# Retention states by full-array products from the second batch on, and the last sums in pieces

## The chip, the cores and the metric

The kernel runs on one core of a Trainium2 chip. The core has five engines with their own instruction streams: PE (TensorE, matrix products into PSUM), DVE (VectorE), ACT (ScalarE), POOL (GpSimd) and SP (SyncE, here only for transfers), and 16 DMA engines. The metric is the device time of one execution in microseconds, as a median of several. Engines work in the order of their streams and wait for each other through semaphores.

## The reference

Two layers follow each other: a recurrent retention over 768 steps and 8 heads, then an MLP mixer with a token part and a channel part. There are 4 batches; a head has 64 columns.

```python
gamma = 1.0 - 2.0 ** (-5.0 - np.arange(H))                 # one decay per head
for t in range(S):                                          # S = 768
    state = gamma[None, :, None, None] * state + np.einsum('bhd,bhe->bhde', k[:, :, t], v[:, :, t])
    y[:, :, t] = scale * np.einsum('bhd,bhde->bhe', q[:, :, t], state)
x  = y.transpose(0, 2, 1, 3).reshape(B, S, H * D)           # 4 x 768 x 512
h  = np.maximum(x.T @ w_tok1, 0) @ w_tok2                   # per batch, along the tokens, 256 wide
u  = x + h.T
h2 = np.maximum(u @ w_ch1, 0) @ w_ch2                       # along the channels, 1536 wide
out = u + h2
```

## The kernel before

The 768 steps are cut into 6 chunks of 128. Two heads form a pair (4 pairs a batch), so that a pair fills the 128 partitions. `front(b, p)` does a pair of a batch: it scales k by powers of gamma, transposes k and q, forms the states at the chunk borders, the scores inside a chunk, the retention output y, and then the token MLP of these 128 channels; its last product is the transposed u (`uT`). `back(b)` does the channel MLP of a batch from the four `uT`: `widen` (384-column products, L803, Relu on ACT) and `narrow` (512-column products, L845) or, for batches 2 and 3, `narrow_seven` (256-column products, L922), which saves one product in eight by sums and differences formed on DVE.

No order of instructions is written down. Every step is an `Op` with an engine (or a choice of engines), an estimated cost, the steps it depends on, and the buffers it takes from a limited number (`BUFS`) or PSUM banks from a range (`BANKS`). A list scheduler in the kernel places them, with some random changes from seeds, and the best order is emitted. Costs in the code are in nanoseconds: (time to the next instruction, time to the result). In the first 36 us products with zeros (L1049, "filler") are put where PE would stand idle.

```python
BUFS = dict(kf=6, qf=6, k16=3, v16=8, kT=4, qT=4, U=2, q16=3, r16=3, am=8, X=3, x16=5, h1=3, u16=3,
            uT=3, h2=2, o=4, w1=2)
BANKS = dict(first=range(0, 7), front=range(0, 5), back=range(3, 8), seven=range(0, 8), fill=range(7, 8))
QR, QH, TN = (0,), (1,), 2
SEEDS = [30004]
...
def front(b, p):
    first, last = b == 0, b == 0 and p == NP - 1
    turned = first and p >= TN            # these pairs take a shortcut to uT, see below
    FA = "first" if first else "front"
    ...
    ST, US, RS = Slot(FA), Slot("U"), Slot("r16")
    def emit():
        st = tile_of(ST, [P, 512], FP)
        for c in range(NC - 1):           # 5 chunk borders
            for j in range(2):            # 2 heads: 10 products into the two halves of the partitions (L527)
                nc.tensor.matmul(st[j * D:(j + 1) * D, c * D:(c + 1) * D], K.tile[:, c, j],
                                 V.tile[:, j, c], start=True, stop=True)
    pp = op(one("PE", (375, 525), emit), kl + [vl, two_before], [ST], [K, V])
    for c in range(NC - 1):               # U[c] = decay * U[c-1] + state product c, on DVE
        def emit(c=c):
            o = ST.tile[:, c * D:(c + 1) * D]
            if c == 0:
                U = tile_of(US, [P, NC - 1, D], FP)
                nc.vector.tensor_copy(U[:, 0], o)                                   # L536
            else:
                U = US.tile
                nc.vector.scalar_tensor_tensor(U[:, c], U[:, c - 1], gp[:, p:p + 1], o,
                                               ALU.mult, ALU.add)                  # L539
    ...                                   # r16 = U scaled, per head on the diagonal blocks (L550/L552)
    ...                                   # scores (L576), mask (L590), y (L606, L610), X (L624/L628), x16 (L641)
    t1: 12 products x16, wt1 (L655);  h1 = relu
    if turned:                            # uT straight from h1 and x16, and the residual later in narrow
        2 x 2 products of 384 columns (L680) and 2 x 3 of 128 (L683), evicted to uT (L690)
        return
    t2: 12 products of 128 columns (L713); X += t2 on DVE, twice (L720); u16 = cast (L728)
    uT: 6 transposes on PE (L747) and an eviction (L753), or a DMA transpose for batches 2 and 3 (L737)
    ...
def narrow(sh):                           # batch 0: the token residual of the turned pairs, 2 products in each of 6 groups
    nc.tensor.matmul(A.tile[:, TN * P:], wt2[:, jt, t], h1_all[:, jt, TN * P:], ...)   # L835
    ...
def narrow_seven():                       # the end of group i
    p7 = mm(PB, lo, ...)
    u3 = add(W1, lo, ...)                                                           # w<-w,bank
    p2 = mm(PA, lo, ...)
    p3 = mm(PC, hi, sv("S4"), b_of(1, 1), False, True, ...)                         # the last 6 products
    ol1 = add(OL, lo, ...)
    oh = op(either(emit, DVE=(640, 700), POOL=(1250, 1330)), [oh, u3], [], [OH, W1]) # OH += W1, 512 wide (L964)
    ol2 = add(OL, hi, ..., [p3, v12], ...)                                          # 256 wide
    stores = [(1, OH, slice(0, C), [oh]), (0, OL, slice(0, C), [ol1, ol2])]
    if b == B - 1 and i == HC - 1:
        stores[1:] = [(0, OL, lo, [ol1]), (0, OL, hi, [ol2])]                       # all from ACT
```

Of the kernel before, what the change touches and what calls it, by code (L numbers as in the profile page):

```python
# [18 lines left out]
def kernel(  # L19
# [32 lines left out]
    BUFS = dict(kf=6, qf=6, k16=3, v16=8, kT=4, qT=4, U=2, q16=3, r16=3, am=8, X=3, x16=5, h1=3, u16=3,  # L52
# [4 lines left out]
    QR, QH, TN = (0,), (1,), 2  # L57
    SEEDS = [30004]
# [31 lines left out]
    def replay(order):  # L90
# [23 lines left out]
        while n:  # L114
# [51 lines left out]
            for e, o in on:  # L166
# [4 lines left out]
                if left[e] <= 0:  # L171
                    left[e] = None
                    dmas[e].pop(0)
                    o.end = t + LAND[e] + (AFTER if e == "POOL" and t > 50000 else 0)
                    n -= 1
# [248 lines left out]
    def front(b, p):  # L424
# [96 lines left out]
        ST, US, RS = Slot(FA), Slot("U"), Slot("r16")  # L521

        def emit():
            st = tile_of(ST, [P, 512], FP)
            for c in range(NC - 1):
                for j in range(2):
                    nc.tensor.matmul(st[j * D:(j + 1) * D, c * D:(c + 1) * D], K.tile[:, c, j],  # L527
                                     V.tile[:, j, c], start=True, stop=True)
        pp = op(one("PE", (375, 525), emit), kl + [vl, two_before], [ST], [K, V])
        prev = None  # L530
        for c in range(NC - 1):
            def emit(c=c):
                o = ST.tile[:, c * D:(c + 1) * D]
                if c == 0:
                    U = tile_of(US, [P, NC - 1, D], FP)
                    nc.vector.tensor_copy(U[:, 0], o)  # L536
                else:
                    U = US.tile
                    nc.vector.scalar_tensor_tensor(U[:, c], U[:, c - 1], gp[:, p:p + 1], o,  # L539
                                                   ALU.mult, ALU.add)  # L540
            prev = op(one("DVE", (190, 273), emit), [pp, prev], [US] if c == 0 else [],
                      [ST, US] if c else [ST])

        def emit(e, j):
# [4 lines left out]
            if e == "ACT":  # L549
                nc.scalar.mul(RS.tile[r, :, r], US.tile[r], g128[2 * p + j])  # L550
            else:
                nc.vector.tensor_scalar(RS.tile[r, :, r], US.tile[r], g128[2 * p + j], None, ALU.mult)  # L552
# [230 lines left out]
    def back(b):  # L783
# [79 lines left out]
        def narrow_seven():  # L863
# [47 lines left out]
            for i in range(HC):  # L911
# [5 lines left out]
                def mm(bank, cols, lhs, rhs, opens, adds, deps, reads):  # L917
# [6 lines left out]
                    return op(one("PE", (648, 806), emit), deps, [bank] if opens else [],  # L924
                              reads + ([] if opens else [bank]))

                def add(o, cols, a, c, deps, takes, uses, pooled=False, n=N2):
# [4 lines left out]
                    cost = dict(DVE=(640, 700) if n > N2 else (365, 425))  # L932
                    if pooled:
                        cost["POOL"] = (1250, 1330) if n > N2 else (720, 800)
                    return op(either(lambda e: emit(e), **cost), deps, takes, uses)
                xl = [x_done[b, p, 0] for p in range(NP)]
# [20 lines left out]
                p3 = mm(PC, hi, sv("S4"), b_of(1, 1), False, True,  # L957
# [125 lines left out]
```

## Time and profile before

| | |
|---|---|
| time, median of 3 | 200.04 us (199.78 to 203.64) |
| span of the profiled execution | 197.7 us |
| granted PE clock | 0.996 |
| PE, weight loads, DVE, ACT, POOL busy | 95%, 66%, 67%, 56%, 41% |
| chain that ended last: PE, DMA, DVE | 62%, 16%, 12% |
| longest part of it, by line | PE L803 24%, L922 13%, L845 12% |
| stores of 256 KB and of 128 KB, issue to landing | 3.0 us, 2.0 us |

The profile is of one execution. A busy engine is one with an instruction under way; matmuls are pipelined, so the time that one costs in a stream is read from the starts of neighbours and not from its own duration. The groups name line, engine, operation, written and read tiles, shape and count, then busy time, mean duration in ns, and the idle time of the engine before them. A chain of work goes back from the last instruction, at each step to what released it. A timeline lists start, duration, engine, line and how many instructions of a kind were merged.

### The profile page before, as it was taken

Reading aid. Unit: us, or ns where it says so; the run is one execution under the profiler, and the core shown is the slowest. Engines: PE = TensorE matmul, PEld = TensorE weight load, DVE = VectorE, ACT = ScalarE, POOL = GpSimd, SP = SyncE. Lnnn points to the kernel's source line nnn. Section 1 sums busy time; section 2 is a strip of 40 time slices with the busy share of each in tenths; the row PEclk is TensorE's granted clock in tenths of the full one; section 3 lists DMA queues with packets and bytes.
Section 4 is the critical chain, followed back from the end, with each engine's and each line's share of the span. In section 5 each row is a group of like instructions: output and inputs, shape, how many; then the busy total and the mean of one; then the engine's idle time right before and its main releaser. Section 6 shows DMA issues by size and latency. Waiting matters only on the chain.

```text
span 197.7 us, 4974 instructions
## 1 busy us (share of the span) xinstructions
PE 188.0 (95%) x1994; PEld 129.8 (66%) x1994; DVE 131.9 (67%) x343; ACT 111.1 (56%) x244; POOL 80.4 (41%) x114
## 2 busy tenths in 40 slices
PE   7778899999999999999999999999999999999991
PEld 3456686666767656667755764567767787667881
DVE  6699671019799997687668425476399687048972
ACT  4468766899758656469460872439765004775000
POOL 7996765389979874246251220222220010000000
PEclk9999999999999999999999999999999999999998
DMA  7999999999999999999999993452220024000232
GB/s 114 149 170 178 209 204 206 179 155 153 145 145 180 109 167 188 149 172 179 153 131 190 157 170 73 120 122 40 40 45 0 0 107 189 26 0 3 100 114 106
DMA packets 97511, 24.89 MB, mean 126 GB/s; under 512 B 90193, under 2 KB 94545, under 8 KB 97489
## 3 DMA queue, kind: packets, MB, share of 16 engines
q0 software_dynamic: 73136, 13.18, 95.3%
q1 hardware_dynamic: 20752, 5.11, 20.4%
q10 hardware_dynamic: 3600, 6.29, 9.8%
q8 instruction: 15, 0.25, 0.6%
q14 instruction: 8, 0.06, 0.1%
HBM read 26.74 MB, written 6.29 MB: 167 GB/s over the span
## 4 chain that ended last, share of the span: by engine, by line
PE 62%; DMA 16%; DVE 12%; POOL 4%; issue 2%; ACT 2%; DVEq 0%; POOLq 0%
PE bank L803 24%; PE bank L922 13%; PE bank L845 12%; DMA wc<-in_moe_w_ch_dram 9%; DMA kf<-in_k_dram 7%; PE bank L655 3%; PE bank L713 3%; DVE am L590 3%; PE bank L576 2%; PE bank L610 2%; DVE U L539 2%; POOL v L387 2%; DVE X L720 1%; DVE k L467 1%; PE bank L606 1%
## 5 line engine op out<-in xcount | busy, mean ns | idle before, releaser
L803 PE MATMUL bank<-uT,wc 128*128 128x384 f16 x384 | 67.9, 326 | 0.0
L817 ACT ACTIVATE h<-bank 128x384 f16<-128x384 f32 x96 | 45.8, 490 | 20.2 <-PE bank L803 14.3
L803 PEld LDWEIGHTS <-wc 128*128 128x128 f16 x384 | 35.7, 98 | 21.5
L590 DVE TENSOR_TENSOR am<-bank,mask 128x384 f16<-128x384 f32 x64 | 32.6, 548 | 10.3 <-PE bank L576 10.3
L845 PE MATMUL bank<-wc,h 128*128 128x512 f16 x144 | 36.2, 380 | 0.0
L624 ACT ACTIVATE X<-bank,gy 128x192 f32<-128x192 f32 x56 | 19.9, 419 | 17.4 <-PE bank L610 17.1
L641 POOL CAST x<-X 128x384 f16<-128x384 f32 x24 | 12.2, 510 | 27.2 <-ACT X L624 24.6
L728 POOL CAST u<-X 128x384 f16<-128x384 f32 x25 | 12.8, 524 | 23.7 <-DVE X L720 23.1
L720 DVE TENSOR_TENSOR X<-X,bank 128x384 f32<-128x384 f32 x28 | 14.3, 549 | 10.2 <-PE bank L713 10.1
L845 PEld LDWEIGHTS <-h 128*128 128x128 f16 x144 | 12.4, 98 | 10.5
L539 DVE SCALAR_TENSOR_TENSOR U<-U,gp,bank 128x64 f32<-128x64 f32 x64 | 17.6, 276 | 1.2
L387 POOL DMA_DIRECT2D v<-in_v_dram x16 | 16.5, 1031 | 4.4 <-DMA kf<-in_k_dram 2.2
L387 POOL DMA_DIRECT2D kf<-in_k_dram x15 | 15.3, 1021 | 2.2 <-DMA qf<-in_q_dram 0.9
L922 PEld LDWEIGHTS <-h 128*128 128x128 f16 x144 | 14.1, 98 | 1.8
L550 ACT ACTIVATE r<-U 64x320 f16<-64x320 f32 x28 | 13.1, 467 | 3.4 <-DVE U L539 3.0
L610 PEld LDWEIGHTS <-am 128*128 128x128 f16 x192 | 12.3, 98 | 2.5
L610 PE MATMUL bank<-v,am 128*128 128x64 f16 x192 | 13.8, 193 | 0.0
L655 PE MATMUL bank<-x,wt 128*128 128x128 f16 x192 | 13.5, 219 | 0.2 <-DVE am L590 0.2
L655 PEld LDWEIGHTS <-wt 128*128 128x128 f16 x192 | 11.9, 98 | 2.7 <-issue 0.5
L467 DVE TENSOR_SCALAR k<-kf,gk 128x384 f16<-128x384 f16 x14 | 6.2, 447 | 10.5 <-DMA kf<-in_k_dram 10.5
L713 PEld LDWEIGHTS <-wt 128*128 128x128 f16 x168 | 10.5, 98 | 2.6 <-issue 0.5
L713 PE MATMUL bank<-h,wt 128*128 128x128 f16 x168 | 12.0, 219 | 0.1
(91 smaller groups left out, 265.9 us busy)
## 6 DMA issues: line engine op xcount, KB each, us to landing
out_dram<-o ACTq DMA_DIRECT2D x23, 256.0 KB, 3.0
v<-in_v_dram POOLq DMA_DIRECT2D x16, 192.0 KB, 8.7
wc<-in_moe_w_ch_dram POOLq DMA_DIRECT2D x6, 512.0 KB, 15.6
kf<-in_k_dram POOLq DMA_DIRECT2D x15, 192.0 KB, 8.6
qf<-in_q_dram POOLq DMA_DIRECT2D x12, 192.0 KB, 8.7
wt<-in_moe_w_tok_dram POOLq DMA_DIRECT2D x2, 384.0 KB, 9.1
qf<-in_q_dram POOLq DMA_DIRECT2D x8, 96.0 KB, 8.4
X<-in_k_dram SPq DMA_DIRECT2D x1, 384.0 KB, 3.5
```

The lines of the kernel that those rows point to most:

```text
L387: nc.gpsimd.dma_start(out=tile_of(s, [P, 2, NC, D], F16), in_=src[b, 2 * p:2 * p + 2].rearrange("h (c p) d -> p (h c) d", p=P))
L539: nc.vector.scalar_tensor_tensor(U[:, c], U[:, c - 1], gp[:, p:p + 1], o, ALU.mult, ALU.add)
L590: nc.vector.tensor_tensor(am[:, :m], src, k_, ALU.mult)
L610: nc.tensor.matmul(o[:, j * D:(j + 1) * D], M.tile[:, m], V.tile[:, j, c], start=(c == 0), stop=(c == 0 or j == 1))
L624: nc.scalar.mul(X.tile[:, half(hf), h * D:(h + 1) * D], yv[:, :, j * D:(j + 1) * D], gy[:, h:h + 1])
L655: nc.tensor.matmul(acc[:, jt * P:(jt + 1) * P], wt1[:, i, jt * P:(jt + 1) * P], X16.tile[:, i], start=(i == 0), stop=(i == NC - 1))
L713: nc.tensor.matmul(acc[:, i * P:(i + 1) * P], wt2[:, jt, t], H1.tile[:, jt], start=(jt == 0), stop=(jt == NJ - 1))
L720: nc.vector.tensor_tensor(xo, xo, T2.tile[:, :HC * P].rearrange("p (i d) -> p i d", d=P), ALU.add)
L803: nc.tensor.matmul(acc[:, :SH], w[:, ct, (ft % FW) * P:(ft % FW + 1) * P], UT.tile[:, ct, sh * SH:(sh + 1) * SH], start=(ct == 0), stop=(c ...
L817: nc.scalar.activation(H2.tile[:, ft], A.tile[:, :SH], AF.Relu)
L845: nc.tensor.matmul(A.tile, H2.tile[:, ft, i * P:(i + 1) * P], wc2[ft // FW][:, ft % FW], start=(opens and ft == 0), stop=(ft == NF - 1), s ...
L922: nc.tensor.matmul(bank.tile[:, cols], lhs(f, t), rhs(f), start=(f == 0 and not adds), stop=(f == HF - 1), skip_group_check=adds)
```

## The change

From batch 1 on (`UNT = 1`), a pair's state at a chunk border is formed by one product of 128 stationary and 128 moving columns, both heads at once, instead of two products of half the array width. Of its four 64 x 64 blocks two mix the heads and are never used; the U sums carry them along, so U is twice as wide (`UW = P`) and the products fill two PSUM banks instead of one. The aim is fewer, fuller products and no change of the array's tiling. Batch 0 keeps the ten half products. To make room, q gets five buffers and x16 four. `TN` goes from 2 to 3, so that only pair 3 of batch 0 takes the shortcut. In the very last group, the last product and its sum are done in two pieces of 128 columns with a store each, the add of W1 is split between POOL and DVE, and the 256 KB store goes out from SP. Other seeds are tried for the order, so all streams after about 28 us are interleaved differently.

```diff
-    BUFS = dict(kf=6, qf=6, ... x16=5, ...)
+    BUFS = dict(kf=6, qf=5, ... x16=4, ...)
...
+    UNT, UW = 1, P
-    QR, QH, TN = (0,), (1,), 2
-    SEEDS = [30004]
+    QR, QH, TN = (0,), (1,), 3
+    SEEDS = [20002, 20003, 20007, 20226]
...
+        whole = b >= UNT
+        STS = [ST, Slot(FA)] if whole else [ST]
+        W = P if whole else D
+        def st_of(c):
+            return STS[c // 4] if whole else ST
...
             for c in range(NC - 1):
-                for j in range(2):
-                    nc.tensor.matmul(st[j * D:(j + 1) * D, c * D:(c + 1) * D], K.tile[:, c, j],
-                                     V.tile[:, j, c], start=True, stop=True)
-        pp = op(one("PE", (375, 525), emit), kl + [vl, two_before], [ST], [K, V])
+                if whole:
+                    nc.tensor.matmul(st_of(c).tile[:, c % 4 * P:(c % 4 + 1) * P],
+                                     K.tile[:, c].rearrange("p h d -> p (h d)"),
+                                     V.tile[:, :, c], start=True, stop=True)
+                else:
+                    ...                                     # the two half products, as before
+        pp = op(one("PE", (270, 420) if whole else (375, 525), emit), kl + [vl, two_before], STS, [K, V])
...
-                    nc.vector.scalar_tensor_tensor(U[:, c], U[:, c - 1], gp[:, p:p + 1], o,
+                    nc.vector.scalar_tensor_tensor(U[:, c, :W], U[:, c - 1, :W], gp[:, p:p + 1], o,
                                                    ALU.mult, ALU.add)
...
-                nc.scalar.mul(RS.tile[r, :, r], US.tile[r], g128[2 * p + j])
+                nc.scalar.mul(RS.tile[r, :, r], US.tile[r, :, r if whole else slice(0, D)], g128[2 * p + j])
...
+                ends = b == B - 1 and i == HC - 1
+                for cols in ((slice(N2, N2 + P), slice(N2 + P, C)) if ends else (hi,)):
+                    p3.append(mm(PC, cols, sv("S4"), ...))
...
+                if ends:
+                    ohs = [op(either(lambda e, hs=hs, f=emit: f(e, hs), **c), [oh, u3], [], [OH, W1])
+                           for hs, c in ((slice(0, 1), dict(POOL=(720, 800))), (slice(1, 2), dict(DVE=(365, 425))))]
...
+                if ends:
+                    store(0, i, OL, lo, [ol1])
+                    store(1, i, OH, slice(0, C), ohs, "SP")
+                    for n_, (p3_, cols) in enumerate(zip(p3, (slice(N2, N2 + P), slice(N2 + P, C)))):
+                        ol2 = add(OL, cols, ..., [p3_, v12], [], [OL, PC], n=P)
+                        store(0, i, OL, cols, [ol2], "ACT")
```

## Prediction

> **What bounds the kernel now.** I read the page's part 1 and its 40 slices first, then the chain that ended last in order of time, then the PE timeline around the instructions that change. Part 1 and the rows of PE and DVE:
>
> ```profile
> PE 188.0 (95%) x1994; PEld 129.8 (66%) x1994; DVE 131.9 (67%) x343; ACT 111.1 (56%) x244; POOL 80.4 (41%) x114
> ...
> PE   7778899999999999999999999999999999999991
> ...
> DVE  6699671019799997687668425476399687048972
> ```
>
> PE is busy in every slice from about 30 us on. As a busy PE isn't PE at its peak, I checked that its matmuls stand end to end. The chain in order of time, its last third:
>
> ```profile
> 144.03 6.50 PE bank L803 x40
> 150.53 3.27 PE bank L922 x30
> 153.81 1.95 PE bank L803 x12
> 155.76 10.48 PE bank L922 x96
> 166.24 13.65 PE bank L803 x84
> 179.89 11.80 PE bank L922 x108
> 191.71 0.69 DVE o L931
> ```
>
> Forty products of 384 columns in 6.50 us are 0.1625 us each, and 108 of 256 columns in 11.80 us are 0.109: the columns at 2.4 GHz plus some 2.5 ns. Nothing waits here. From the chain and the timeline I take for one full-array product of 128 columns 0.056 us (twelve L655 in 0.67). The first L803 starts at 30.68 us; from there to the last PE product, streaming and mode changes explain all but about half a microsecond of some 163. So the kernel is bound by PE's work after 30.7 us, by what comes before that (loads and dependences), and by a tail of 4 us. PE work removed after 30.7 us comes off the time almost one to one; other engines matter only where they make PE wait.
>
> **What the state products cost.** The PE timeline around one pair's ten products (L527):
>
> ```profile
> 96.54 0.49 PE L803 MATMUL bank<-uT,wc 128*128 128x384 f16 x2
> 96.96 0.35 PE L527 MATMUL bank<-v,k 128*64 128x64 f16 x10
> 97.24 0.50 PE L803 MATMUL bank<-uT,wc 128*128 128x384 f16 x2
> ```
>
> The two L803 should have streamed by 96.54 + 2 x 0.1625 = 96.86, yet L527 starts at 96.96: 0.10 us of gap. The ten themselves take 97.24 - 96.96 = 0.28 us. The 0.38 in all recurs at the other pairs of later batches.
>
> **What the Trainium skill says.** "TensorEngine Tiling (Array Packing)", Key Properties: "Changing tiling mode (not just tile) drains the TensorE". The trace agrees: 0.10 us when the half-width products come after full-width ones. "TensorE: Matmul & The Clock Gate", "Wait — 56ns, not 53.3ns?": 128 columns take 55.6 ns back to back; the trace's 56 agrees. "VectorE: DVE Perf Modes", "Why PSUM operands drop a tier": fp32 operands in PSUM run at one element per cycle. The trace agrees: DVE adds of 256 and 512 columns take 417 and 688 ns (below), 1.06 ns a column. "DMA: Bandwidth & Descriptors", Anatomy of one DMA, puts about 2 us of fixed cost on a transfer; the page's part 6 has stores of 256 KB landing after 3.0 us and of 128 KB after 2.0, so here size counts as well.
>
> **The change part by part.**
>
> 1. State products. Five full-array products of 128 columns: 5 x 0.056 = 0.28 us, with no change of mode. Streaming is thus the same; what goes is the 0.10 us of gap, in 12 pairs (batches 1 to 3): 12 x 0.095 = **-1.13 us** of PE.
>
> 2. The threshold TN goes from 2 to 3: pair 2 of batch 0 no longer goes through the transposed shortcut. PE loses 4 products of 384 (0.65), 6 of 128 (0.34), and in the six narrow groups of batch 0, 12 products shrink from 256 to 128 columns (12 x 0.053 = 0.64). It gains 12 L713 (0.67) and 6 transposes (0.34). Net **-0.62 us** of PE. In exchange DVE gets two adds (L720, 0.47 us each start to start) and POOL two casts.
>
> 3. DVE. The rows:
>
> ```profile
> L539 DVE SCALAR_TENSOR_TENSOR U<-U,gp,bank 128x64 f32<-128x64 f32 x64 | 17.6, 276 | 1.2
> L931 DVE TENSOR_TENSOR o<-o,bank 128x256 f32<-128x256 f32 x6 | 2.5, 417 | 0.3 <-PE bank L922 0.2
> L931 DVE TENSOR_TENSOR o<-X,bank 128x512 f32<-128x512 f32 x6 | 4.1, 688 | 1.0 <-PE bank L922 0.8
> ```
>
> Five instructions a pair get 64 more columns: 5 x 64 x 1.06 = 0.34 us, +4.1 us of DVE over 12 pairs. Where does DVE have no room? By stages of 10 us (columns: PE, PEld, DVE, ACT, POOL busy):
>
> ```profile
> 50.00:60.00 10.00, 9.87 (x135) 6.73 (x134) 8.74 (x23) 5.97 (x13) 8.41 (x11) 1.00 3.63 145
> 60.00:70.00 10.00, 9.82 (x123) 6.63 (x121) 9.77 (x26) 7.43 (x14) 9.20 (x11) 1.00 2.48 145
> ```
>
> So it lies in the front of batch 1, where the chain runs through DVE too (about 52 to 70 us). PE has batch 0's channel MLP to fill in with and didn't wait. The widening of batch 1 starts at 85.1 us; its last transposed input is evicted at 79.7 to 80.2. The changed order asks for it earlier: between the first widening product of batch 0 and that of batch 1 stand 50.5 us of PE work instead of 53.7, so it is due near 81.5. Adding up DVE's instructions from the first scaling of k in batch 1 to the last L720 of that batch gives 26.2 us before and 26.0 after: the scheduler moved other DVE work behind it. So it should hold, with a microsecond to spare instead of five. I put **+0.3 us** on waits of this kind, two PSUM banks per state included.
>
> 4. The head. Until the second L713 group the streams are identical. Then pair 2's L713 group stands where L680 started at 28.54:
>
> ```profile
> 28.54 0.49 PE L680 MATMUL bank<-wt,h_all 128*128 128x384 f16 x2
> ...
> 29.86 0.98 PE L655 MATMUL bank<-x,wt 128*128 128x128 f16 x12
> 30.68 1.14 PE L803 MATMUL bank<-uT,wc 128*128 128x384 f16 x6
> ```
>
> 28.54 + 0.67 = 29.21; six transposes until about 29.67; three filler products until 30.16; L655 waits for a DVE cast that now stands behind pair 2's first add (about 30.2). It starts near 30.3 and not 29.86, so the first L803 near 31.0, with 0.32 us less work done before it (14.64 against 14.96): **+0.6 us** of idle PE.
>
> 5. The tail. The end of the timeline:
>
> ```profile
> 193.55 1.33 ACTq L973 DMA_DIRECT2D out_dram<-o  x3
> 193.76 0.41 DVE L931 TENSOR_TENSOR o<-o,bank 128x256 f32<-128x256 f32 x1
> ```
>
> Three stores were issued one after the other on ACT, some 0.45 us apart; the last at about 194.45, although its add ended at 194.18. After: the 256 KB store goes to SP, but ACT still issues three (128, 64, 64 KB). The first can't go before the left add, which ends 0.3 us earlier as the add with W1 is split between POOL and DVE. The last issue thus stays near 0.7 us after PE's end; the saved part is mostly the smaller last transfer, against the later POOL half (0.73 us). **-0.15 us**.
>
> Sum: -1.13 - 0.62 + 0.3 + 0.6 - 0.15 = -1.0 us, so 200.04 - 1.0 = **199.0 us**.
>
> **Rivals.** (a) DVE becomes the bound in batch 1: each microsecond by which the last input of the widening comes after 81.5 us is one of PE. For it: 9.77 of 10 us busy between 60 and 70. Against it: equal DVE sums to the deadline, and PE's filling work. It would give 200 to 202. (b) The gain is full: no new wait, and the head loses nothing because the filler products only stood where PE waited anyway. Then -1.13 - 0.62 - 0.3 = -2.0, or 198.0. For it: PE waited only half a microsecond after 30.7 us in a schedule made in the same way. (c) The mode changes don't vanish but move: the score products (L576, 64 rows) are left as they are, so where L527 stood directly next to them a gap was shared. In batches 1 to 3 none of the L527 groups stands next to L576 in the trace, so I count nothing. It would halve part 1: 199.6. (d) Fewer buffers (qf 5, x16 4) hold up the POOL queue, which issues loads in order. A load of batch 2 would then wait for a transpose of batch 1 long done; up to +1 us, only if a weight or a k comes late.
>
> **Range and chances.** The gains are counted products with measured durations; the uncertain terms (head, waits, tail) are each some tenths, and rival (a) has a tail upward. 198.0 to 200.7 should hold it 8 times in 10. Faster by over 2% would need 4 us, more than all removed work: 0.02. Slower by over 2% needs a new wait of 5 us: 0.04. Within 2%: 0.94.
>
> **What would show it.** In the profile after: the state products as 60 full-array ones, five in 0.28 us with no gap ahead; U updates of 128 columns about 340 ns long; first L803 equivalent near 31.0 us; the first widening product of batch 1 at 81 to 82 us without a PE wait ahead; PE's last product near 192.9 us; a span near 196.7. I'm wrong if PE waits for DVE or for transposed inputs between 50 and 85 us or near 152 us (batch 3's inputs), if a gap stays at the state products, or if the head differs by over a microsecond.

## The result and the profile after

| | before | after |
|---|---|---|
| time, median of 4 | 199.91 us (199.52 to 203.64) | 197.77 us (197.54 to 198.15) |
| ratio, with 95% interval | | 0.9901 [0.9874, 0.9929] |
| profiled execution: time, span | 199.45, 197.7 us | 198.15, 196.4 us |
| first widening product of batch 0 | 30.68 us | 30.75 us |
| first widening product of batch 1 | 84.93 us | 81.39 us |
| last product of PE starts | 193.37 us | 192.04 us |
| from there to the end of the span | 4.31 us | 4.34 us |

The four executions are faster by 1.0%, about twice what was predicted, and the time lies below the predicted range. First the page of the kernel after, part 1 and the slices of PE and DVE:

```profile
PE 187.0 (95%) x1951; PEld 130.6 (67%) x1951; DVE 132.1 (67%) x338; ACT 112.9 (58%) x251; POOL 82.9 (42%) x118
...
PE   7878899999999999999999999999999999999991
...
DVE  6699682017899998677676726566299686048972
```

PE has 43 instructions fewer, and as before it is busy in every slice from 30 us on. DVE's busy time is the same within 0.2 us in spite of the wider sums. PE's timeline of the kernel after around one pair's state products (L536):

```profile
43.18 0.49 PE L818 MATMUL bank<-uT,wc 128*128 128x384 f16 x2
43.51 0.44 PE L536 MATMUL bank<-v,k 128*128 128x128 f16 x5
43.78 0.65 PE L818 MATMUL bank<-uT,wc 128*128 128x384 f16 x3
```

Two widening products of 0.1625 us from 43.18 have streamed by 43.51, where the five state products start; 0.28 us later the next product starts. The 0.10 us of gap that stood ahead of the ten half products is gone. It is so at every pair: ahead of the twelve groups of batches 1 to 3, the trace before has eleven gaps of 0.093 to 0.095 us and one of 0.133, 1.17 us in all, and the trace after has none above 0.001. The score products with 64 rows, which were left as they are, have a gap of 0.096 us ahead of each of their twelve groups in both traces, so the gaps have not moved there, as rival (c) had it. Over the whole run I summed the time by which each product of PE starts later than its predecessor has streamed, from the first widening product to the last product: 4.39 us before, 3.26 after. (The level depends on the streaming time taken for the half-array products, the difference does not.) The twelve gaps thus account for the whole difference of 1.13 us, and PE's other waits sum to the same in both traces within 0.04 us.

The sums of the states, from the costliest groups of the page:

```profile
L553 DVE SCALAR_TENSOR_TENSOR U<-U,gp,bank 128x128 f32<-128x128 f32 (+1 forms) x64 | 20.9, 327 | 1.5
```

The 327 ns are a mean over two shapes: 48 sums of 128 columns at 345 ns and 16 (batch 0) of 64 columns at 272.

The head, in PE's timeline of the kernel after:

```profile
29.52 0.65 PE L1086 MATMUL bank<-zero 128*128 128x384 f16 x3
30.01 0.90 PE L670 MATMUL bank<-x,wt 128*128 128x128 f16 x12
30.75 0.81 PE L818 MATMUL bank<-uT,wc 128*128 128x384 f16 x4
```

The three filler products (L1086) run from 29.52 to 30.01, and T1 (L670, the first product of the token MLP) starts there: it does not wait for the cast.

### The profile page after: what moved, and what is told of

Same layout as the page of the kernel before. It is cut to its first block, busy times and chain, and to the rows that moved or that the text cites. A ratio compares the mean times of both kernels' runs of the same rounds, so it can differ in the third digit from the quotient of the medians.

```text
span 196.4 us, 4910 instructions
## 1 busy us (share of the span) xinstructions
PE 187.0 (95%) x1951; PEld 130.6 (67%) x1951; DVE 132.1 (67%) x338; ACT 112.9 (58%) x251; POOL 82.9 (42%) x118
## 4 chain that ended last, share of the span: by engine, by line
PE 73%; DMA 12%; DVE 6%; POOL 3%; issue 2%; ACT 1%; ACTq 0%; DVEq 0%; POOLq 0%
PE bank L818 32%; PE bank L937 14%; PE bank L860 9%; DMA qf<-in_q_dram 9%; PE bank L670 4%; PE bank L728 4%; DMA kf<-in_k_dram 3%; DVE am L605 3%; PE bank L591 2%; PE bank L625 2%; PE bank L502 1%; PE bank L621 1%; PE bank L536 1%; DVE U L553 1%; POOL v L388 1%
## 5 line engine op out<-in xcount | busy, mean ns | idle before, releaser
L818 PE MATMUL bank<-uT,wc 128*128 128x384 f16 x384 | 69.3, 326 | 0.0
L656 POOL CAST x<-X 128x384 f16<-128x384 f32 x25 | 12.8, 513 | 29.8 <-ACT X L639 25.9
L639 ACT ACTIVATE X<-bank,gy 128x192 f32<-128x192 f32 x58 | 20.6, 420 | 6.1 <-PE bank L625 5.9
L735 DVE TENSOR_TENSOR X<-X,bank 128x384 f32<-128x384 f32 x30 | 15.8, 550 | 9.9 <-PE bank L728 9.7
L553 DVE SCALAR_TENSOR_TENSOR U<-U,gp,bank 128x128 f32<-128x128 f32 (+1 forms) x64 | 20.9, 327 | 1.5
L743 POOL CAST u<-X 128x384 f16<-128x384 f32 x27 | 13.4, 516 | 17.9 <-DVE X L735 17.7
L564 ACT ACTIVATE r<-U 64x320 f16<-64x320 f32 x31 | 14.5, 467 | 5.9 <-DVE U L553 5.5
L990 POOL TENSOR_TENSOR o<-o,w 128x256 f32<-128x256 f32 x1 | 1.0, 964 | 32.2 <-DVE w L947 32.2
L670 PE MATMUL bank<-x,wt 128*128 128x128 f16 x192 | 13.6, 219 | 0.5 <-DVE am L605 0.3
L670 PEld LDWEIGHTS <-wt 128*128 128x128 f16 x192 | 11.9, 98 | 2.6 <-issue 0.9
L728 PE MATMUL bank<-h,wt 128*128 128x128 f16 x180 | 13.3, 219 | 0.0
L728 PEld LDWEIGHTS <-wt 128*128 128x128 f16 x180 | 11.5, 98 | 2.5 <-issue 0.2
## 6 DMA issues: line engine op xcount, KB each, us to landing
wc<-in_moe_w_ch_dram POOLq DMA_DIRECT2D x6, 512.0 KB, 15.2
```

What stands on the lines that cost most here:

```text
L553: nc.vector.scalar_tensor_tensor(U[:, c, :W], U[:, c - 1, :W], gp[:, p:p + 1], o, ALU.mult, ALU.add)
L639: nc.scalar.mul(X.tile[:, half(hf), h * D:(h + 1) * D], yv[:, :, j * D:(j + 1) * D], gy[:, h:h + 1])
L670: nc.tensor.matmul(acc[:, jt * P:(jt + 1) * P], wt1[:, i, jt * P:(jt + 1) * P], X16.tile[:, i], start=(i == 0), stop=(i == NC - 1))
L728: nc.tensor.matmul(acc[:, i * P:(i + 1) * P], wt2[:, jt, t], H1.tile[:, jt], start=(jt == 0), stop=(jt == NJ - 1))
L735: nc.vector.tensor_tensor(xo, xo, T2.tile[:, :HC * P].rearrange("p (i d) -> p i d", d=P), ALU.add)
L818: nc.tensor.matmul(acc[:, :SH], w[:, ct, (ft % FW) * P:(ft % FW + 1) * P], UT.tile[:, ct, sh * SH:(sh + 1) * SH], start=(ct == 0), stop=(c ...
```

## Experiments

Times are medians with the lowest and highest execution; ratios are to the kernel before on the same chip, with a 95% interval. The ratios leave out executions more than 1.5% above the fastest of their kernel, so they can differ from the ratio of the medians.

### Are the products' gains what the gap says?

**Ten half-array products and 64-column sums again, in the new order.**

```diff
-                if whole:
-                    nc.tensor.matmul(st_of(c).tile[:, c % 4 * P:(c % 4 + 1) * P],
-                                     K.tile[:, c].rearrange("p h d -> p (h d)"), V.tile[:, :, c], ...)
-                else:
+                if True:                                    # the two half products, in all batches
...
-                nc.vector.scalar_tensor_tensor(U[:, c, :W], U[:, c - 1, :W], ...)
+                nc.vector.scalar_tensor_tensor(U[:, c, :D], U[:, c - 1, :D], ...)
```

> The changed kernel's order of instructions on every engine, but in batches 1 to 3 the states again by ten half-width products, with U 64 wide. Theory (PE-bound, the gap of a change of tiling costs 0.095 us a pair): 1.1 us above the changed kernel, and a gap of 0.10 us ahead of each of the 12 groups. Rival (the gain comes from the other order of the scheduler and from TN, not from the states): within 0.3 us of the changed kernel. Rival (DVE's wider U costs time): less than 0.8 us above, as DVE gets back 4 us.

Measured: 200.01 us (199.36 to 201.61), 1.0009 [0.9993, 1.0026]. So the order, `TN` and the new end seem to bring nothing alone. But PE's timeline shows a wait that the changed kernel does not have:

```profile
58.28 0.60 PE L856 MATMUL bank<-wc,h 128*128 128x512 f16 x2
59.76 0.45 PE L666 MATMUL bank<-x,wt 128*128 128x128 f16 x5 [0.88 <-DVE U L549]
```

T1 waits for the last sum of a pair, and 1.05 us pass between the streams. In this version all five states of a pair lie in one PSUM bank; in the changed kernel the fifth is in a second bank, so I take it that the bank T1 needs comes free one sum earlier there. The sum on DVE is what the trace names; the bank is my reading of the code. It fits that in the changed kernel T1 starts ahead of that last sum:

```profile
58.60 0.83 PE L670 MATMUL bank<-x,wt 128*128 128x128 f16 x12
...
59.44 0.34 DVE L553 SCALAR_TENSOR_TENSOR U<-U,gp,bank 128x128 f32<-128x128 f32 x1
```

The wait is thus one of this experiment, which keeps an order made for two banks. Without it the version would stand near 199.0 us (an estimate, 200.01 less 1.05), so it doesn't show that the rest of the change brings nothing.

**Ten full-stationary products of 64 columns**: the count of the old kernel with the tiling of the new.

```diff
                 if whole:
-                    nc.tensor.matmul(st_of(c).tile[:, c % 4 * P:(c % 4 + 1) * P], K..., V.tile[:, :, c], ...)
+                    for j in range(2):
+                        nc.tensor.matmul(st_of(c).tile[:, c % 4 * P + j * D:c % 4 * P + (j + 1) * D], K..., V.tile[:, j, c], ...)
```

> Order of the changed kernel; each of the five full products as two of 64 moving columns with the whole stationary matrix: ten products and ten weight loads, the same columns streamed, no change of tiling. Theory (tiling change is what costs): as the changed kernel, within 0.3 us, no gap ahead of the group, ten in 0.28 us or little more. Rival (the number of products and weight loads costs): 1 us or more above, ten taking 0.37 us or more.

Measured: 199.67 us (198.13 to 203.41), 0.9972 [0.9946, 0.9997]; the spread is the subject of a later part. Its traced execution took 202.99 us at a granted clock of 0.987, so only the places of its products are read. PE's timeline at a pair:

```profile
72.46 0.59 PE L861 MATMUL bank<-wc,h 128*128 128x512 f16 x2
72.89 0.45 PE L537 MATMUL bank<-v,k 128*128 128x64 f16 x10
73.18 0.59 PE L861 MATMUL bank<-wc,h 128*128 128x512 f16 x2
```

Two products of 512 columns of 0.215 us from 72.46 end at 72.89, where the ten start; they take 0.29 us. No gap, although there are ten; at eleven of the twelve pairs there is none, at one 0.05 us. What the change saves is the change of tiling and not the number of products.

### The end

**The old end of the last sums** (DVE adds all of the right half, no pieces, stores from ACT):

```diff
-                ends = b == B - 1 and i == HC - 1
+                ends = False
```

> The changed kernel with the old end: last product in one piece, W1 added at once on DVE, all three last stores from ACT. Prediction: 0.15 us slower than the changed kernel. From the trace (last product's end to the end of the span 4.20 us before, 4.29 after): 0.05 to 0.1 us faster, since ACT still issues three stores one after the other and the last one goes at the same distance from PE's end.

Measured: 199.29 us (197.48 to 201.20), 0.9946 [0.9922, 0.9971]. The median says little, again because of the spread, but in the trace the last product is followed by 4.29 us to the end of the span, against 4.34 and 4.32 in two traces of the new end. The new end saves nothing.

**The very last piece stored from SP** instead of as the third issue on ACT (with the moved loads of the version with late k and v below):

```diff
-                        store(0, i, OL, cols, [ol2], "ACT")
+                        store(0, i, OL, cols, [ol2], "SP" if n_ else "ACT")
```

> The first variant of this call, and the very last piece's store goes out from SP, so that ACT issues two stores at the end instead of three. The last ACT issue started 1.10 us after the last product's start with DVE done at 0.74. Theory: the last issue starts near 0.8 us, the end comes 0.25 to 0.35 us earlier: 197.5 to 197.9. Rival (the end is set by the transfers, not by the issues): no difference.

Measured: 199.53 us (197.83 to 201.76), 0.9946 [0.9913, 0.9979]; from the last product to the end 4.32 us, no change. So the third issue on ACT isn't what ends the kernel. In the timeline of the kernel after, the end is:

```profile
191.47 0.96 POOL L990 TENSOR_TENSOR o<-o,w 128x256 f32<-128x256 f32 x1 [32.16 <-DVE w L947]
...
192.21 1.32 ACTq L955 DMA_DIRECT2D out_dram<-o  x3
...
192.46 0.36 SPq L955 DMA_DIRECT2D out_dram<-o  x1
```

The 256 KB store (SPq) can't go before POOL's half ends, at 192.43. It goes 0.42 us after the last product's start (192.04); before, it went first from ACT, 0.18 after. It is not the last to land, though: it is through at 194.64, and the third store of ACT at 195.15. That one is issued 1.10 us after the last product's start, before as after, and its size doesn't matter here. Stores of the end, KB each and us to landing, before and then after:

```profile
out_dram<-o ACTq DMA_DIRECT2D x2, 128.0 KB, 2.0
```

```profile
out_dram<-o ACTq DMA_DIRECT2D x2, 64.0 KB, 2.1
```

The very last took 1.91 us with 128 KB and 2.02 with 64. With its issue from SP, 0.23 us earlier, it landed 3.11 us after the last product's start, as in the changed kernel. So at the end the landings are what counts; that the later 256 KB store holds up the small ones behind it is likely and not shown.

### Has DVE room?

**One more copy of 128 columns on DVE for each state sum** (five a pair, into a tile that nobody reads):

```diff
                     nc.vector.scalar_tensor_tensor(U[:, c, :W], U[:, c - 1, :W], ...)
+                if whole:
+                    nc.vector.tensor_copy(dump, o)
```

> The changed kernel with one more DVE copy of 128 x 128 beside each state sum of batches 1 to 3 (0.2 us each, 1 us a pair, three times what the change itself added), otherwise the same order. Prediction's rival (DVE near its limit in batch 1): PE waits appear between 70 and 85 us, 2 us or more above the changed kernel. My reckoning (DVE had about a microsecond to spare): about 1 to 3 us above. If DVE has wide slack: within 0.5 us.

Measured: 201.12 us (200.67 to 202.37), 1.0053 [1.0028, 1.0078]. DVE is busy 141.2 us instead of 132.1, some 0.8 us a pair more, and PE's gaps sum to 6.6 us instead of 3.26. After 31 us PE waits for the extra copy to read its bank, a wait that the changed kernel does not have:

```profile
PE bank L594 <- DVE dump L557: 0.7, 2, 0.4
...
PE bank L765 <- DVE dump L557: 0.2, 1, 0.2
```

Beside them stand 0.3 us for a sum on DVE and 0.5 for a Relu on ACT. So a bound by DVE, rival (a), is near: over twice the change's own 0.34 us a pair is too much, while that 0.34 still fits.

### The spread

**The changed kernel again**, and later four more traces of it.

> The changed kernel again, for a second trace and a narrower interval. By the trace in hand the span fell 1.3 us (1.13 of it the gaps at the state products, the rest other PE work) while the medians fell by 2.1. If the trace is typical, the difference narrows to 1.3 to 1.6 us (ratio 0.992 to 0.9935). If the trace in hand was one of the slower executions of the changed kernel, the difference stays near 2 us (0.989 to 0.991) and the new trace shows where, most likely before the first widening product (30.75 us so far).

Measured: 199.41 us (197.74 to 199.94), 0.9957 [0.9925, 0.9989]. The eleven times are 197.74, 197.90, 198.00, 198.27, 198.37 and then 199.41 to 199.94: two groups with nothing between. The four recorded times all lie in the lower one. The four later traces:

> The changed kernel once more, for its trace. Holding back the scaling of k did not remove the upper group of executions, so its cause is open. If this execution falls into the upper group (199.3 us or more), its trace shows where it departs from the lower one: before the first widening product (beyond 31.2 us: the loads at the start), between 50 and 85 us (a PE wait of 1 to 2 us), or later. If it is of the lower group (197.5 to 198.6), it repeats the traces in hand.

> As the first run of this call, the changed kernel for another trace. Upper group: one of the three places; lower group: first widening product at 30.7 to 31.2 us and no PE wait above 0.4 us after it.

> As the first run of this call, the changed kernel for another trace. Upper group: one of the three places; lower group: first widening product at 30.7 to 31.2 us and no PE wait above 0.4 us.

> As the first run of this call, the changed kernel for another trace. Upper group: one of the three places; lower group: first widening product at 30.7 to 31.2 us and no PE wait above 0.4 us.

Measured: 199.71, 200.75, 199.48 and 199.68, all in the upper group or above it, at a granted clock of 0.995 to 1.0 as in the lower. All four ran on one chip, and the eleven above on another, so the group may go with the chip; that was not tried. Now the upper group can be read. Its own PE gaps sum to 5.4 to 5.8 us against 3.26 and 3.10 in the two traces of the lower group. In the first of them the 2.31 us over the recorded trace are 0.70 at 41 to 45 us, about 1.1 between 75 and 78, and 0.5 between 82 and 84. The first cancels against the head: in this trace the first widening product stands at 29.97 us, 0.8 earlier than in the recorded one, and PE then gives it back in waits, 0.3 us of them for a load of q. The rest is the upper group's loss. In the waits of ACT between 70 and 86 us, first the recorded trace, then the first of the four:

```profile
ACT k L466 <- DMA kf<-in_k_dram: 1.1, 1, 1.1
ACT q L475 <- DMA qf<-in_q_dram: 0.9, 1, 0.9
```

```profile
ACT k L466 <- DMA kf<-in_k_dram: 2.1, 1, 2.1
...
ACT q L475 <- DMA qf<-in_q_dram: 1.4, 1, 1.4
```

DVE waits for its half of the same k: 0.5 us in the recorded trace, 1.6 in the other. These are k and q of batch 2's last pair, issued by POOL at 60.5 and 61.5 us in both. k landed 14.0 us later in the recorded trace and 15.0 in the other, q 18.1 and 19.7 us later. Loads of this size issued between 36 and 60 us take 7 to 9. What stands behind them in ACT's stream, in the recorded trace and then in the upper one:

```profile
79.67 0.83 ACT L475 COPY q<-qf 128x768 f16<-128x768 f16 x1 [0.89 <-DMA qf<-in_q_dram]
...
80.41 1.35 ACT L639 ACTIVATE X<-bank,gy 128x192 f32<-128x192 f32 x4
```

```profile
81.20 0.83 ACT L475 COPY q<-qf 128x768 f16<-128x768 f16 x1 [1.41 <-DMA qf<-in_q_dram]
...
81.94 1.35 ACT L639 ACTIVATE X<-bank,gy 128x192 f32<-128x192 f32 x4
```

The copy of q (L475) stands in ACT's stream ahead of the four adds to X of batch 2's first pair (L639). They need nothing from it, but wait for it: 80.41 against 81.94. POOL's casts of that X and T1 (L670) follow. POOL is held by the same landing, because the kernel issues a load only when the one eight places earlier has landed, and the casts of X stand behind such an issue. POOL's timeline, in the same two traces:

```profile
79.94 1.01 POOL L388 DMA_DIRECT2D kf<-in_k_dram  x1 [2.98 <-DMA qf<-in_q_dram]
81.26 1.06 POOL L656 CAST x<-X 128x384 f16<-128x384 f32 x2 [0.30 <-ACT X L639]
```

```profile
81.48 1.02 POOL L388 DMA_DIRECT2D kf<-in_k_dram  x1 [3.50 <-DMA qf<-in_q_dram]
82.79 1.06 POOL L656 CAST x<-X 128x384 f16<-128x384 f32 x2 [0.30 <-ACT X L639]
```

From here theory A is that engines working in order behind these two late loads make the upper group. The rivals are other causes that only go along with it.

### Taking work out from behind the late loads

All of these only move entries of the finished order; the code marks k, q, their transposes and the loads of a pair, and `later(what, mark, n)` moves the marked entries to the place of the entry that fits `mark`, or n places further.

**k of the pair later** (its scaling and its transpose), alone and with the issue of v of batch 3's second pair:

```diff
+    later([("k", 2, 3), ("kT", 2, 3)], lambda o_: o_.prio == (0, 2, 3, 3))
+    later([("v16", 3, 1)], lambda o_: o_.nm == ("kf", 3, 2))       # only in the version with both
```

> As the previous, but the v load stays ahead of the two casts in POOL's stream. If POOL's stop at that load matters of itself: a part of the slow executions stays, median 198.3 to 199.3. If only the scaling of k holds up batch 1: like the previous, 197.8 to 198.2.

Measured: 198.50 us (197.72 to 201.32), 0.9932 [0.9902, 0.9962]; eleven executions up to 198.56, nine from 199.62 up.

> The executions of the changed kernel fall into two groups, near 198.0 and near 199.7 us. In a slow execution's trace (of the variant with ten full products) the scaling of k of batch 2, pair 3, which stands in ACT's and DVE's streams ahead of work for batch 1, waited 5 us for its load, which landed 18.6 us after its issue; POOL also stood 3.9 us at a load issue ahead of two casts. Here the same instructions, but this scaling and its transpose stand behind batch 1's last adds and evictions, and one v load is issued after those casts instead of before. Theory (the late k load holds up batch 1's end and so PE): the upper group goes, median 197.8 to 198.2. Rival (the upper group comes from elsewhere, such as the head or the slower transposes): two groups as before, median 198.8 or above.

Measured: 199.32 us (197.63 to 202.88), 0.9930 [0.9903, 0.9956]. Both missed: the first keeps the two groups, and the second's executions are spread without a clear gap. Theory A would explain it thus: q lands after k, and at a time that the queue sets, so without the wait for k the engines reach the copy of q earlier and wait there longer. That is not shown, as no upper execution of the two was traced. The traced ones, 198.26 and 198.69, have no wait behind k or q. The 198.69 is the head's doing: its first widening product stands at 31.76 us, and from there to the last product it takes 160.84, 0.1 more than the version with both later, below. So the head is a second source of spread.

**k and q of the pair later**, with the issue of k of batch 3's third pair, all behind the two casts of X of batch 2's first pair:

```diff
+    later([("k", 2, 3), ("kT", 2, 3)], lambda o_: o_.prio == (0, 2, 3, 3))
+    later([("q", 2, 3), ("qT", 2, 3), ("kf", 3, 2)], lambda o_: o_.prio == (0, 2, 0, 22), 1)
+    later([("v16", 3, 1)], lambda o_: o_.nm == ("kf", 3, 2))
```

> The changed kernel with five things moved behind the two POOL casts of x of batch 2's first pair (the last place in front of T1 of batch 2): the scaling of k of batch 2 pair 3 and its transposing, the copy of q of that pair and its transposing, the issue of k of batch 3 pair 2; the issue of v of batch 3 pair 1 moves there too. Nothing is computed otherwise. Theory A: the upper group of executions (199.4 to 199.9) is DVE, ACT and POOL standing in order behind the late landing of k and q of batch 2 pair 3 (k landed at 75.3 to 75.5 us in the upper traces and at 74.5 in the lower, q at 81.0 to 81.2 against 79.6; ACT's copy of q, L475, waited until then, and ACT's adds, POOL's casts and T1 came after it). Expected: one group only, median 197.3 to 198.2, no execution of the settled kind at 199.4 or above; between 74 and 85 us under 0.5 us of PE waits. Rival B: the upper group has another cause (loads late for other consumers, or the chip): still two groups, some 197.7 and 199.6, about half of the executions in each. Rival C: moving the q transposes back only moves the wait to the scores of that pair near 90 us: one group or two near 199.

Measured: 197.69 us (197.61 to 198.63, 6 executions), 0.9896 [0.9870, 0.9922]. No upper group in these six, nor in six of the same version with the old end below; the next version, with q alone, does have executions over 199.4 us on the same chip. The traced execution is the best evidence, because its loads came as late as in the upper group: k 15.0 us and q 19.6 us after the issue. Yet PE's gaps sum to 2.69 us, and between 70 and 86 us PE waits for no other engine. ACT's timeline:

```profile
80.14 0.73 ACT L648 ACTIVATE X<-bank,gy 128x192 f32<-128x192 f32 x2 [0.19 <-PE bank L634]
81.26 0.83 ACT L478 COPY q<-qf 128x768 f16<-128x768 f16 x1 [0.39 <-DMA qf<-in_q_dram]
```

The adds (now L648) are through before the copy waits for q at 81.26.

**Only q later**:

> Only the copy of q of batch 2 pair 3, its transposing and the issue of k of batch 3 pair 2 are moved behind the two POOL casts of x of batch 2's first pair; the scaling of k stays where the changed kernel has it. Theory A: the first half of the upper group's loss stays (DVE and ACT wait for k of pair 3 to 75.5 us, some 1.0 to 1.2 us of PE waits between 75 and 78), the second half (1.0 us of PE waits at 82 to 84) goes: groups near 197.6 and 198.7, median 197.6 to 198.8. Rival B: no effect, groups at 197.7 and 199.6, median near 199. Moving the k alone left both groups in place, which theory A explains by q's landing being the later of the two and fixed by the queue: then the q move does more than the k move.

Measured: 198.66 us (197.59 to 201.85), 0.9935 [0.9909, 0.9961]; twelve of twenty executions between 197.98 and 198.99, as theory A had it, but six from 199.47 up, which theory A does not explain and of which there is no trace. Its trace again has the late landings (15.2 and 19.8 us). The gaps ahead of T1 at 82 us are gone, those at 76 to 78 are there, 1.4 us in five pieces, and ACT waits 2.2 us for k. So each load has its own half of the loss.

**The half products with the same moves**:

> The ten half-array state products and the sums 64 wide in all batches, in the order of the changed kernel, with the same moves as the late k and q version. It stands against that version as the products alone do, without the wait behind the late loads. Theory A: no two groups either, and 1.13 us (twelve gaps of 0.094) plus 0.2 to 0.3 (streaming) above the late k and q version: median 198.7 to 199.6, so 1.1 to 1.5 us above. If the products' gain is eaten by the longer sums on DVE, the two versions lie within 0.4 us of each other.

Measured: 200.12 us (199.53 to 200.98), 0.9996 [0.9970, 1.0021]: 2.4 us above the version with full products, which is more than expected. Between the first widening product and the last product it takes 163.04 us against 160.72. Of these 2.32 us, 1.05 are the wait of T1 for the last state sum that was seen above, 0.14 smaller waits, and the remaining 1.13 the twelve gaps, read one by one. The sums on DVE ate none of the gain. The 1.05 us are what the second bank is worth in this order, if my reading of the bank is right; an order made for one bank need not have that wait, as the kernel before shows.

**k and q later and the old end**:

> The late k and q version with the old end of the last sums (DVE adds the whole right half, no sums in pieces on POOL), meant to be the fastest. Theory A with an end that is 0.03 to 0.1 us cheaper: median 197.2 to 198.1, one group, 0 to 0.15 us under the late k and q version. If the new end does save its predicted 0.15 us, it is 0.15 us above that version. Rival B: two groups again.

Measured: 197.55 us (197.46 to 198.14), 0.9883 [0.9857, 0.9910], the fastest of all. Its end takes 4.30 us from the last product, 0.04 less than the changed kernel's.

### Why do these loads land late?

**The transposes later, k and q of the last pair where they were.** SP's transposes of batch 2 go through the same DMA engines. In the trace of the half products with the same moves they start 1.4 us later, and there k landed 10.1 us after its issue and q 13.7.

```diff
+    later([("q", 2, 0), ("qT", 2, 0), ("kT", 2, 0)], lambda o_: o_.prio == (0, 1, 1, 30), 1)
```

> The changed kernel with the copy of q of batch 2 pair 0, its DMA transpose and that of k moved behind one cast of u on DVE (and so all of SP's transposes later by some 1.4 us: the first starts near 62.2 instead of 60.84); k and q of pair 3 stay in their places of the changed kernel. Theory T: the loads of k and q of batch 2 pair 3 (issued at 60.5 and 61.5) land late because the transposes' packets of 256 bytes take turns with the loads' packets on the same DMA engines from 64 us on, so what counts is how much of these loads is through by then. In the half-array version the transposes started 1.4 us later and k and q landed at 71.1 and 75.6 instead of 74.5 to 75.5 and 79.6 to 81.2. Expected: k lands by 72.5 and q by 77.5, DVE and ACT no longer wait for them over 0.3 us, one group of executions, median 197.4 to 198.2. Rival U: the landing doesn't depend on when the transposes start (the loads are slow for their own reason): k at 74.5 to 75.5, two groups as in the changed kernel, 197.8 and 199.6. Rival V: the later q and k of pair 0 make the scores of batch 2 wait instead: one group near 199.

Measured: 198.22 us (198.01 to 198.79, 6 executions), 0.9930 [0.9902, 0.9957]. Only the copy of q of batch 2's first pair on DVE and the first two transposes on SP are moved, and with them the transposes behind: the first is issued at 62.85 us instead of 60.84. k is issued at 60.5 as before and lands after 9.2 us instead of 14.0 or more (the k tile, instructions issued between 60.2 and 61.3 us):

```profile
L388 POOL DMA_DIRECT2D kf<-in_k_dram x1: 1037/1037/1037, 60.5 to 60.5; - x1
...
DMA to landing us min/median/max: 9.2/9.2/9.2
```

No engine waits for it, and q lands after 14.6 us, 76.1 on the clock, before it is needed. No second group in six executions, though the changed kernel was not run beside them on that chip. The 0.5 us that this version is behind the one with k and q later are new PE waits near 64 and 66 us, for the mask work of DVE that was pushed back.

The Trainium skill ("DMA: Bandwidth & Descriptors", Queues, rings and completion order) says that a DMA engine takes turns between the queues that have work, packet by packet. The traces agree. Counted in the recorded trace of the kernel after, the loads' queue moves 2,451 packets between 62 and 64 us, before the transposes' packets come, and 518, 479 and 540 in each 2 us from 68 to 74, where the transposes' queue moves 532, 483 and 511: nearly one for one. The load packets are of 127 bytes on average and the transposes' of 245.

All twenty traces of this case fit. In the five where the first transpose is issued at 61.96 us or later, k of batch 2's last pair is there by 69.7 to 71.6; in the fifteen where it is issued earlier, at 72.3 to 78.7. What counts seems to be the time on the clock and not the distance to the load's own issue: in the trace of k and v moved, everything stood some 1.1 us later, the transposes were issued 0.3 us behind k as in the recorded trace, and k landed after 8.0 us. Within the fifteen the transposes' start does not order the landings.

### The kernel before, traced once more

> The kernel before, unchanged, traced once more. Its recorded trace was of an execution at 199.45 us, 0.5 us under the median of its 200.0 (some 190 executions). Theory A: a typical execution of it also waits behind late k or q of batch 2, which its recorded trace hardly showed (DVE waited 1.2 us for k, PE 0.8 us in all after 30.7 us): if this one is at 199.8 us or above, the PE waits between 60 and 85 us sum to 0.5 us or more over the first trace's. Rival B: the difference lies in the head or is spread over the whole: no such waits. If the execution comes in at 199.5 or below, it tells nothing.

Measured: 199.93 us, span 198.2; its PE gaps sum to 4.83 us instead of 4.39. The difference is near 50 and 53.5 us (the wait inside a T2 group is 0.62 us instead of 0.30), and not at late loads of batch 2: k landed after 10.9 us. This one trace speaks against the part of theory A that concerned the kernel before. Why DVE is later there in this execution wasn't tried.

## Why the prediction was wrong, by its own steps

| step | predicted | measured in the recorded trace |
|---|---|---|
| 1. state products | -1.13 | -1.17 (the twelve gaps) |
| 2. `TN`, work after the first widening product | -0.30 | -0.27 (162.69 to 161.29, less all gaps) |
| 3. waits behind DVE and the like | +0.3 | +0.04 here (the rest of the gaps); +1.3 to +2.6 of span in the four later traces |
| 4. head, first widening product | +0.3 | +0.07 |
| 5. tail | -0.15 | +0.03 |
| sum | -1.0 | -1.3 (spans 197.7 to 196.4) |

**Step 1 was right**, and ten full products of 64 columns without a gap show that its reason, the change of tiling, is right too. **Step 2** was right: its 0.62 us are the 0.30 in the table and the 0.32 of work that left the head. The value in the table is what remains after the gaps, as `TN` wasn't tried alone.

**Step 3 failed.** It put +0.3 us on the waits of batch 1, the two PSUM banks included, as one number. The runs show two values: 0.04 us in the recorded trace, and some 1.8 us more in six of a later eleven executions. The cause it named, DVE's longer sums, was not it. The loads of batch 2 were: two of them shared the DMA engines with the transposes, and three engines stood in order behind their landing. Rival (d) had named a load of batch 2 that comes late, and "up to +1 us only if a weight or a k comes late"; it gave it the wrong size (1.3 to 2.6 us), and for a reason, fewer buffers, that no run tested alone. 199.0 lies in the gap between the two groups, where hardly any execution of this kernel falls. Rival (b), the full gain, 198.0, is nearest to the recorded time, but by luck: it took 2.0 us off, and the traces differ by 1.3.

**Step 4 was mis-sized.** It expected T1 to wait for a cast until 30.3 us. T1 started when the filler products ended, at 30.01, and the first widening product stood at 30.75 instead of 31.0. That is 0.25 us. The step also had the six transposes end at 29.67, though its own 0.34 us for them lead to 29.55; the trace has 29.52.

**Step 5 had the wrong sign.** It counted on the smaller last transfer, and that saved nothing: 64 KB took 2.02 us to land and 128 KB had taken 1.91. The longer time of 256 KB stores in part 6 is a median over the run; at the end, before, such a store landed in 2.07 us. The step took POOL's half of the add for 0.73 us; it took 0.96, and the 256 KB store behind it went out 0.24 us later than before. The three issues on ACT, which the step held to be the limit, are not: taking one away changed nothing.

The steps are only a part of the miss. Of the 1.3 us between 199.04 and 197.77 they make 0.3: steps 3 and 4 half a microsecond, of which step 5 takes back 0.2. Some 0.6 is the base: 200.04 was a median, and the terms came from one execution of 199.45; the second trace of the kernel before has 0.44 us of that as PE waits near 50 us. The last 0.4 is that the traced execution after, 198.15, was the slowest of its four. That all four fell into the lower group was luck: the median of the later eleven, 199.41, lies inside the predicted range.

Two smaller points. The prediction had PE wait half a microsecond after 30.7 us; without the gaps at half-array products the trace has 0.9. And the sharp deadline of the prediction, batch 1's widening near 81.5 us, was right: 81.39, 81.36 with k and q later, and 82.1 to 84.5 in the upper group.

Open stay: what decides, with issue times alike to within 0.1 us, whether the two loads are 1 to 1.5 us later or not; the upper executions of the versions with k or q alone; the effect of `TN` and of the fewer buffers alone.

## What to carry to other kernels

A change that takes work out of the bounding engine moves its consumers closer to the loads, so ask of each late load what stands behind its wait in the order of every engine, even work that doesn't need it; here moving a few entries took away the upper group in twelve executions, some 1.8 us, more than the 1.3 that the change itself gains. Sum a change's gain from one trace, but look at several executions before giving a wait one value: where their times fall into two groups, a trace of each names the wait. Full-array products with unused blocks are a good trade where half-array ones stand between full ones: the gap goes, the streaming stays the same, and DVE paid 0.07 us a sum.

## What the runs showed of the hardware that was not expected

- Loads issued at 60 us took 14 to 20 us instead of 7 to 9 when seven transposes were issued behind and beside them; with the transposes 2 us later k landed after 9.2 us.
- The gap behind full-array products is the same for a half-array stationary of 64 columns (0.093 to 0.095 us in eleven of twelve groups) and of 64 rows (0.095 to 0.096 in all twelve).
- Ten products of 128 rows by 64 columns stream in the time of five of 128 columns (0.29 and 0.28 us), without a gap at either end.
- Two halves of one addition: an add of 128 x 256 f32 in SBUF took 0.96 us on POOL and 0.43 us on DVE at the same time.
- An earlier head is no sure gain: in three traces the first widening product stood 0.8 us earlier, and PE's gaps between 41 and 46 us gave 0.75, 0.6 and 0.2 us of it back.
